# Loading the slices of a first weight with three transfers over 128 partitions in place of four over 32

## Chip, cores and metric

One core of a Trainium2 chip runs the whole kernel. The metric is device time in microseconds (us). Profiles are taken by the hardware profiler, and times in them count from the start of the span, which is some 2 us shorter than the time of a run. PE is the engine of matrix products (PEld is its loading of weights); VectorE (DVE), ScalarE (ACT) and GpSimd (POOL) do the other arithmetic; SP issues the transfers, which 16 DMA engines carry out in packets. A pattern "leads with" the count of its slowest dimension that is not 1.

## The reference

A gated linear attention followed by a feed-forward block. Only the second part touches the change.

```python
# q, k, v, alpha: (4, 8, 768, 48) float32; w_in: (384, 2048), w_out: (2048, 384) float64
for t in range(S):
    state = alpha[:, :, t, :, None] * state + einsum('bhd,bhe->bhde', k[:, :, t], v[:, :, t])
    y[:, :, t] = einsum('bhd,bhde->bhe', q[:, :, t], state)
x = y.transpose(0, 2, 1, 3).reshape(3072, 384)
h = x @ w_in
out = (h * clip(h + 3, 0, 6) / 6) @ w_out
```

The weights come in as float64. The kernel loads the 8 bytes of each number as two 32-bit words and makes float32 of them on ScalarE, VectorE and GpSimd.

## The kernel before

The first weight `w_in` is loaded in eight slices of 256 columns. Row `96 p + 32 t + r` of `w_in` must land in partition `32 p + r` at place `t` (p is a pair of heads, 0 to 3; t is 0 to 2; r is 0 to 31), since the attention leaves x in that order.

```python
    def load_weight(i):
        u = 2 if wide else 1                      # wide: float64 as two words
        dst = weight_dst(i)
        m = dst.shape[1]
        to = raw_of(i).rearrange("p (m n) w -> p m (n w)", m=m) if wide else dst
        if i < NW1:                               # first weight: 8 slices
            n = NSL // KT                         # 256 columns, 2,048 bytes a row
            src = moe_w_in[:, u * i * n : u * (i + 1) * n].rearrange(
                "(p t r) f -> p r t f", p=NP, t=KT)
            for p in range(NP):
                nc.sync.dma_start(out=to[32 * p : 32 * p + 32], in_=src[p])
        else:                                     # second weight: 8 slices, 128 partitions
            o = (i - NW1) * m * C
            nc.sync.dma_start(
                out=to, in_=moe_w_out[o : o + m * C, :].rearrange("(f p) n -> p f n", p=C))
    # ... cut: d1, d2, dx (ScalarE), d3 (VectorE), d4 (GpSimd) turn slice i into float32
```

A hand-made list of words fixes the order in which every engine's work is issued. `w.7` loads slice 7, `d1.7` to `d4.7` convert it, `f.1.7.2` is a product that uses it, `lq.4` loads a tile of q, and `tq.4` transposes it on PE.

```
... w.5 f.0.3.2 sm.3 fg.0.0 ... w.6 f.1.0.0 ... w.7 ca.5 r.5 f.1.2.3 ... d4.5 ... lq.4 fr.0.3 fa.2.0 d3.6 w.8 ...
d3.7 w.9 fr.0.5 tq.4 fr.0.2 f.1.6.3 q.4 d4.7 fg.0.2 d2.8 fg.0.5 d1.8 lk.4 p.5 f.1.7.2 ...
```

## Time and profile before

| | before |
|---|---|
| time, median of 3 runs | 565.23 us (563.75 to 565.41) |
| span of the profiled run | 561.2 us |
| PE busy | 553.9 us, 99% |
| first weight | 8 slices of 786,432 bytes, 4 transfers each, last packet ends at 58.6 us |

(The prediction puts the end of the last packet at 58.9 us. Its times of packets lie some 0.24 us late against the start of the span; here and below they are counted anew from the traces. Differences between them don't change.)

From the page, the count of DMA packets:

```profile
DMA packets 96972, 52.71 MB, mean 94 GB/s; under 512 B 49936, under 2 KB 90128, under 8 KB 96912
```

And busy time by stretch (columns: stretch, its length, then PE, weight loads, VectorE, ScalarE and GpSimd, each busy us and count; then granted clock, DMA share and GB/s):

```profile
14.00:60.00 46.00, 43.46 (x516) 37.02 (x516) 38.02 (x56) 30.37 (x42) 16.05 (x10) 1.00 1.08 187
60.00:100.00 40.00, 40.00 (x326) 31.17 (x326) 35.32 (x52) 22.11 (x32) 15.62 (x15) 1.00 0.67 188
```

While the first weight comes in, PE stands still for only 2.5 of 46 us; from 60 us on it does not stand still at all.

### The profile page before, as it was taken

To read this page: it belongs to the slowest core of one execution; us is meant where nothing else is said; L and a number is where in the kernel's file an instruction comes from. 1 tells how busy PE (TensorE), PEld (TensorE's weight loads), DVE (VectorE), ACT (ScalarE), POOL (GpSimd) and SP (SyncE) were. 2 spreads that over 40 slices of the span, in tenths; PEclk is the share of its full clock that TensorE was granted. 3 is DMA by queue.
4 is the path that set the end of the run, shared out by engine and by line. 5 is a ranking of instruction groups with operands and counts; after the bars stand their busy time and mean duration, and the time that the engine had idled before them with its cause. 6 is when DMAs were issued, how large, how long until landed. Compare 5 with 4: busy or idle time off the path is not lost.

```text
span 561.2 us, 13170 instructions
## 1 busy us (share of the span) xinstructions
PE 553.9 (99%) x5458; PEld 512.6 (91%) x5458; DVE 475.2 (85%) x796; ACT 198.2 (35%) x350; POOL 52.9 (9%) x70
## 2 busy tenths in 40 slices
PE   8899999999999999999999999999999999999997
PEld 7788886699899999999999999899999999999997
DVE  6977997999999999998899899989899886474580
ACT  1567755102521433222342342322332333341420
POOL 2234344100000000000000001000000010000000
DMA  9999856524204606225442551353242400000000
GB/s 147 182 184 205 214 185 179 119 69 110 62 8 117 150 8 158 73 62 137 111 99 51 154 138 34 86 143 86 82 115 60 113 23 1 8 15 15 1 21 30
DMA packets 96972, 52.71 MB, mean 94 GB/s; under 512 B 49936, under 2 KB 90128, under 8 KB 96912
## 3 DMA queue, kind: packets, MB, share of 16 engines
q1 hardware_dynamic: 90288, 47.15, 37.6%
q10 hardware_dynamic: 6624, 4.72, 2.5%
q8 instruction: 43, 0.70, 0.5%
q14 instruction: 17, 0.14, 0.1%
HBM read 43.71 MB, written 8.13 MB: 92 GB/s over the span
## 4 chain that ended last, share of the span: by engine, by line
PE 92%; SPq 3%; DMA 2%; DVE 1%; ACT 1%; issue 0%; POOL 0%; DVEq 0%
PE m_ps L701 35%; PE m_ps L601 32%; PE m_ps L480 6%; PE sc_ps L346 4%; PE y_ps L449 4%; PE m_ps L518 4%; PE y_ps L459 2%; PE m_ps L491 2%; SPq L256 1%; DMA raw<-in_moe_w_in_dram 1%; PE u_ps L413 1%; SPq L267 0%; PE u_ps L419 0%; PE kb_ps L363 0%; SPq L276 0%
## 5 line engine op out<-in xcount | busy, mean ns | idle before, releaser
L701 PE MATMUL m_ps<-w,g_sb 128*128 128x192 f32 x704 | 121.7, 327 | 0.0
L701 PEld LDWEIGHTS m_ps<-w,g_sb 128*128 128x128 f32 x704 | 113.9, 190 | 1.6 <-issue 0.6
L607 ACT COPY g_sb<-m_ps 128x512 f32<-128x512 f32 x110 | 63.9, 584 | 127.5 <-PE m_ps L601 116.4
L701 PE MATMUL m_ps<-rings,g_sb 128*128 128x192 f32 x528 | 91.5, 327 | 0.0
L701 PEld LDWEIGHTS m_ps<-rings,g_sb 128*128 128x128 f32 x528 | 85.4, 190 | 0.3
L601 PE MATMUL m_ps<-xc,w 128*128 128x128 f32 x640 | 84.3, 279 | 0.1
L496 ACT ACTIVATE r<-g_sb,half 128x512 f32<-128x512 f32 x80 | 57.1, 722 | 73.4 <-DVE g_sb L538 27.5
L601 PEld LDWEIGHTS m_ps<-xc,w 128*128 128x128 f32 x640 | 77.4, 192 | 3.5 <-issue 1.4
L500 DVE SCALAR_TENSOR_TENSOR g_sb<-r,g_sb 128x512 f32<-128x512 f32 x80 | 54.9, 692 | 19.7 <-PE m_ps L701 10.8
L396 POOL TENSOR_TENSOR t<-t,R 128x384 f32<-128x384 f32 x20 | 21.1, 1054 | 359.7 <-DVE t L434 165.8
L601 PE MATMUL m_ps<-xT,raw 128*128 128x128 f32 x400 | 52.4, 277 | 0.0
L601 PEld LDWEIGHTS m_ps<-xT,raw 128*128 128x128 f32 x400 | 48.8, 192 | 0.8 <-issue 0.4
L601 PE MATMUL m_ps<-xT,w 128*128 128x128 f32 x320 | 43.0, 279 | 0.0
L648 DVE TENSOR_TENSOR g_sb<-g_sb 128x512 f32<-128x512 f32 (+1 forms) x55 | 41.5, 790 | 0.1
L601 PEld LDWEIGHTS m_ps<-xT,w 128*128 128x128 f32 x320 | 39.1, 191 | 1.6 <-issue 0.6
L352 DVE TENSOR_TENSOR A<-sc_ps,mask 128x512 f32<-128x512 f32 x48 | 30.8, 682 | 8.3 <-PE sc_ps L346 8.3
L480 PE MATMUL m_ps<-xT,w 128*128 128x256 f32 x144 | 32.4, 380 | 0.0
L601 PE MATMUL m_ps<-xc,raw 128*128 128x128 f32 x240 | 32.3, 278 | 0.0
L315 DVE TENSOR_TENSOR_SCAN R<-t,ones 128x516 f32<-128x516 f32 x24 | 29.3, 1219 | 2.0 <-ACT t L306 1.5
L326 DVE TENSOR_TENSOR_SCAN P<-t 128x516 f32<-128x516 f32 x24 | 30.7, 1279 | 0.2
L538 DVE TENSOR_TENSOR g_sb<-g_sb 128x512 f32<-128x512 f32 x40 | 26.9, 685 | 4.5 <-ACT g_sb L607 4.1
L601 PEld LDWEIGHTS m_ps<-xc,raw 128*128 128x128 f32 x240 | 29.7, 192 | 0.8 <-issue 0.4
(112 smaller groups left out, 699.8 us busy)
## 6 DMA issues: line engine op xcount, KB each, us to landing
raw<-in_moe_w_out_dram SPq DMA_DIRECT2D x8, 768.0 KB, 4.7
t<-in_v_dram SPq DMA_DIRECT2D x48, 96.0 KB, 3.0
raw<-in_moe_w_in_dram SPq DMA_DIRECT2D x24, 192.0 KB, 5.7
out_dram<-oh ACTq DMA_DIRECT2D x44, 96.0 KB, 1.7
qq<-in_q_dram SPq DMA_DIRECT2D x36, 96.0 KB, 2.5
aq<-in_alpha_dram SPq DMA_DIRECT2D x36, 96.0 KB, 2.5
kq<-in_k_dram SPq DMA_DIRECT2D x36, 96.0 KB, 2.5
far<-kq SPq DMA_DIRECT2D x13, 256.0 KB, 2.1
```

The costliest lines, as they stand in the source:

```text
L315: nc.vector.tensor_tensor_scan(out=reverse(R, n - 1, n), data0=reverse(ax, n, n), data1=reverse(ones, n, n), initial=0.0, op0=ALU.mult, op ...
L326: nc.vector.tensor_tensor_scan(out=P_t[j], data0=aX[j % 2][:, 0:n], data1=ini[j % 2], initial=0.0, op0=ALU.mult, op1=ALU.add)
L346: nc.tensor.matmul(sc[h % 2][:, h // 2], K_t[j][r, h // 2], Q_t[j][r, h // 2], start=True, stop=True)
L352: nc.vector.tensor_tensor(out=A_t[j][:, NP * o : NP * (o + 1)], in0=ps_t.pop(("sc%d" % o, j)), in1=mask.unsqueeze(1).to_broadcast([C, NP, ...
L480: nc.tensor.matmul(h[:, f], w1[:, kk, o : o + C], xT_t[g][:, kk], start=(kk == 0), stop=(kk == KT - 1))
L496: nc.scalar.activation(out=to, in_=h, func=AF.Relu, bias=half, scale=1.0 / 6.0)
L500: nc.vector.scalar_tensor_tensor(out=to, in0=r, scalar=1.0, in1=h, op0=ALU.min, op1=ALU.mult)
L538: eng.tensor_tensor(out=out, in0=in0, in1=in1, op=ALU.add if s1 > 0 else ALU.subtract)
L601: nc.tensor.matmul(acc[g][i][:, f * C : (f + 1) * C], spots[w][:, f * C : (f + 1) * C], x_of(g, x), start=(first and f == 0), stop=last, s ...
L607: nc.scalar.copy(out=slots[z], in_=acc[g][i])
L648: nc.vector.tensor_tensor(out=out, in0=in0, in1=in1, op=ALU.subtract)
L701: nc.tensor.matmul(to[g], a, rhs[:, f], start=(first and f == 0), stop=(last and f == HF - 1), skip_group_check=True)
```

## The change

The intent: a transfer over all 128 partitions, so that the load isn't held to the DMA ports that 32 partitions reach (point 1 of the prediction below), and three issues a slice in place of four.

```diff
             src = moe_w_in[:, u * i * n : u * (i + 1) * n].rearrange(
-                "(p t r) f -> p r t f", p=NP, t=KT)
-            for p in range(NP):
-                nc.sync.dma_start(out=to[32 * p : 32 * p + 32], in_=src[p])
+                "(p t r) f -> t p r f", p=NP, t=KT)
+            for t in range(KT):
+                nc.sync.dma_start(out=to[:, t], in_=src[t])
```

What the built program carries for one transfer (counts of the dimensions, slowest first): before, source 32 x 3 x 512 and destination 32 x 3 x 512; after, source **4 x 32** x 512 and destination 128 x 1 x 512. The rows of one t lie in four groups 96 rows apart, so the source can't be written as one run of 128 rows.

## The prediction

> **What bounds the kernel now.** I read the page first (busy shares, then the 40 slices).
>
> ```profile
> span 561.2 us, 13170 instructions
> ...
> PE 553.9 (99%) x5458; PEld 512.6 (91%) x5458; DVE 475.2 (85%) x796; ACT 198.2 (35%) x350; POOL 52.9 (9%) x70
> ...
> PE   8899999999999999999999999999999999999997
> DMA  9999856524204606225442551353242400000000
> GB/s 147 182 184 205 214 185 179 119 69 110 62 8 117 150 8 158 73 62 137 111 99 51 154 138 34 86 143 86 82 115 60 113 23 1 8 15 15 1 21 30
> ```
>
> PE is busy nearly all of the time, so a microsecond in which PE stands still early is a microsecond at the end: no later slack can give it back. The DMA row says where PE can be made to wait. Transfers are dense only in the first six or seven slices (14 us each), and there the row is at 9: the front of the kernel already runs near what its transfers deliver. The changed transfers lie in that front. The view of DMA issues gives their number and size, first the before's own:
>
> ```profile
> raw<-in_moe_w_in_dram SPq DMA_DIRECT2D x24, 192.0 KB, 5.7
> ...
> g_sb<-in_moe_w_in_dram SPq DMA_DIRECT2D x8, 192.0 KB, 7.0
> ```
>
> That is 32 transfers of 196,608 bytes, four to each of 8 slices (786,432 bytes a slice, 6.29 MB in all), every packet 2,048 bytes (one row of a slice), so 96 packets a transfer. In the chain of waits, one slice's transfer is on the path itself, the first:
>
> ```profile
> 14.08 7.58 DMA raw<-in_moe_w_in_dram
> ...
> 21.68 0.97 ACT w L207
> ...
> 25.99 1.86 POOL w L228
> ...
> 27.89 1.60 PE m_ps L491 x12
> ...
> 64.46 7.82 PE m_ps L480 x36
> ```
>
> The words read: the slice lands at 21.7, ScalarE and GpSimd turn its float64 bits into float32, and the first product with it starts at 27.9. After 32 us the chain is PE alone. But the timeline shows that PE is only just behind the last slices:
>
> ```profile
> 59.55 0.95 ACT L207 ACTIVATE w<-raw 128x768 f32<-128x768 f32 x1
> ...
> 65.31 1.47 POOL L228 TENSOR_TENSOR w<-raw 128x768 int32<-128x768 int32 x1 [2.75 <-DVE raw L221]
> ...
> 66.83 5.05 PEld L480 LDWEIGHTS m_ps<-xT,w 128*128 128x128 f32 x24 [0.18 <-POOL w L228]
> ```
>
> The eighth slice's last packet ended at 58.9 (packets of the trace); its conversion starts at 59.55, ends at 66.8, and the weight loads at 66.83 waited 0.18 us for just that. So the eighth slice has no slack: if it lands later by X, PE stands still by nearly X. Two stretches give the speed, one filled by first-weight slices, one by second-weight slices (128 partitions each):
>
> ```profile
> 44.00:48.00 4.00, 4.00 (x35) 3.49 (x34) 2.81 (x6) 3.21 (x8) 1.97 (x2) 1.00 1.17 201
> 84.00:88.00 4.00, 4.00 (x60) 3.17 (x59) 3.32 (x7) 3.04 (x5) 1.80 (x2) 1.00 0.84 246
> ```
>
> The last column is GB/s. Within a slice the trace has 96 packets per about 1.0 us, 197 GB/s; second-weight slices, alone in the queue, 201 to 292 GB/s.
>
> **What the Trainium skill says.** (1) "SBUF — State Buffer", section "Door 1: The DMA port swizzle": a transfer that touches 32 neighbouring partitions reaches 8 of the 16 DMA ports (it lists 189 GB/s for 1 MiB there), 128 partitions reach all. The trace agrees: 197 GB/s, and inside a slice most packets take about 160 ns where a lone one takes 84, as if two engines shared a port. This is surely the change's intent. (2) "DMA: Bandwidth & Descriptors", section "Why a DMA increments its semaphore by 16 and not by 1": a transfer issued from SP runs on k engines, k the largest number up to 16 that divides the slowest dimension (not 1) of both access patterns as the instruction carries them; only these k engines post to the semaphore. (3) The same page's "Rules for kernel authors" warns that an outermost dimension under 16 confines the transfer to that many engines. The trace before agrees with (2): its 433 transfers all lead with 32 or 128, and it holds 6,929 packets of 4 bytes, that is 433 x 16 semaphore writes (and one other). (4) "TensorE: Matmul & The Clock Gate", Part 1, says that PE drops to half clock after some 3.4 us idle; the trace agrees in kind: the first matmuls on the identity take 0.25 us each, later ones 0.12.
>
> **The change part by part.** In the built programs the destination becomes 128 partitions x 512 words, but the source, which skips between the four groups of rows, is carried as 4 x 32 x 512. It leads with 4; before, both sides led with 32. By (2), k = 4: engine p carries group p, and 12 engines have no part in the first weight.
> - Removed: 8 of 32 issues on SP, at 0.43 us (median) each, 3.4 us. SP is waiting for earlier landings most of this stretch, so worth about 0.
> - Same: 3,072 packets of 2,048 bytes. No compute instruction is added, removed or reordered: the order of PE, DVE, ACT and GpSimd is the same but for buffer numbers.
> - Each transfer: 128 packets over 4 engines, 32 each. A packet alone takes 84 ns, and an engine runs them end to end (state copies of 2,048-byte packets later in the trace: one begins every 84 ns on each engine). 32 x 84 = 2.7 us a transfer, 8.1 us a slice, 98 GB/s in place of 197 (4.0 us a slice).
> - The queue on these four engines from 14.5 us, when the first slice's packets start, to the end of the eighth: 8 slices x 8.1 = 64.5 us; between them nine transfers of k, q, v and alpha tiles (q3, k3 and the like, 196,608 bytes each, both halves of a v counted as one, and the last q tile comes after). At the 163 GB/s of the first 14 us each takes 1.2 us on all 16 engines, and the four busy ones serve it in their turn: about 9 x 1.2 = 10.8. Sum 75.3, so the eighth slice ends at 89.8 us. The same sum for before, 32 x 1.0 + 10.8 + 14.5 = 57.3, is 1.6 under the 58.9 seen, so the method holds.
> - On the path: the eighth slice is 31 us later. Its conversion took 7.2 us in before amid other work, some of it will now be done while waiting; alone it is ScalarE 0.93 + DVE 0.69 + 0.69 + 0.96 + GpSimd 1.47, with a second ScalarE pass 5.7. So PE's f.1.7 products move from 67.0 to about 96.5, by 29 to 30 us. The steps before show the same in smaller: slice 1 lands +2, slice 0 +7 (its first product at 37.7 moves by 5), slice 2 puts PE at +13, slice 5 at +19, slice 6 at +24.
> - After it: the second weight (16 engines, paced by conversion, 4 us a slice) starts some 31 us later too, and its last slice has about 3 us of slack before its product, so nothing is added. PE's bursts between waits are 4 us against waits of 5, so it will often be cold; only the last warm-up is not hidden, about 2 us.
> Sum: 565.2 + 29.5 + 2 = about 597.
>
> **The rivals.**
> A. All 16 engines carry it after all (the two patterns are matched in some other way). Then a slice goes at 250 to 290 GB/s, 2.9 us as the second weight's. The first slice lands perhaps 2 to 4 us sooner in a stretch where PE already waits; the rest is hidden, since PE is the chain after 32 us. 560 to 564 us. For it: it is the intent. Against it: the source's leading 4, and the rule that the trace agrees with so far. 12%.
> B. k = 4 at full speed per engine, as summed: about 590 to 605. 50%.
> C. k = 4, and the engines also get in each other's way: engines 0 and 1 would write partitions 0-31 and 32-63, which by (1) are the same 8 ports, in the same order. If two step together, each packet takes the 160 ns seen in before, a slice up to 15.4 us, and the eighth slice ends at 14.5 + 123 + 11 = 148: +90 us, 655. An engine that is four packets (0.34 us) ahead is out of the other's way, and engines in this trace drift by more than that, so I expect a part of it at most. For it: the 160 ns. 30%.
> D. k = 4 but mostly hidden, because PE does other work first: 570 to 585. Against it: PE runs its words in a fixed order, and the 0.18 us wait. 8%.
>
> **Range and chances.** The sum gives 597; some weight of C raises the point to 600. 8 in 10: 578 to 650, from D's upper end to most of C. Faster by over 2% (under 554) would need more than rival A gives: 2%. Within 2%: A and a little of D, 13%. Slower: 85%.
>
> **What would show it.** The page's packet total tells k by itself: 96,972 now; with k = 4 the semaphore packets fall from 32 x 16 to 24 x 4, giving about 96,556; with k = 16 about 96,844. If I am right, GB/s in the slices from 14 to 90 us falls to about 100 to 130, dense transfers reach to 125 us in place of 95, time to landing of the first weight doubles or more (5.7 to over 11 us), and the chain of waits shows the first weight's DMA and its conversion several times between 30 and 97 us, with PE busy 5% less than all. A 2,048-byte packet near 84 ns means B, near 160 means C. I am wrong if the slices run at over 190 GB/s (A), or if they are slow and PE yet starts its products at 67 us (D).

## The result, and the profile after

| | before | after |
|---|---|---|
| time, median | 564.5 us (4 runs) | 594.1 us (593.5 to 594.8, 4 runs) |
| ratio | | 1.0524, 95% interval 1.0500 to 1.0548 |
| span of the profile | 561.2 us | 591.7 us |

Ratios here and below are from runs of the same rounds, and not quite the ratios of the medians quoted. The result is correct and the kernel slower by 5.2%, by the forecast's own mechanism, a fuller queue on four engines. The page of the kernel after:

```profile
span 591.7 us, 13144 instructions
...
PE 561.0 (95%) x5458; PEld 518.7 (88%) x5458; DVE 472.9 (80%) x796; ACT 197.9 (33%) x350; POOL 52.0 (9%) x70
...
PE   8775687999999999999999999999999999999998
...
PEclk9988888999999999999999999999999999999999
DMA  9433337644430071523544255045224230000000
GB/s 146 113 110 108 113 113 195 216 120 122 111 95 8 30 196 36 128 57 93 130 113 95 67 140 141 18 119 139 74 76 106 58 80 8 2 14 21 1 20 28
DMA packets 96556, 52.71 MB, mean 89 GB/s; under 512 B 49520, under 2 KB 89712, under 8 KB 96496
```

Read the last line first. The bytes are the same, but there are 416 packets fewer. Before, the 32 transfers of the first weight each ended in 16 semaphore packets of 4 bytes, 512 in all; 512 - 416 = 96 = 24 x 4. So each of the 24 new transfers runs on four engines. The row of GB/s says the same: from the second slice to the sixth it lies at 108 to 113, where it was 182 to 214. PE's row has its holes in these slices and the seventh, in which the first weight ends, and nowhere after. By stretch:

```profile
14.00:60.00 46.00, 31.20 (x435) 26.76 (x436) 24.03 (x37) 18.69 (x28) 9.27 (x7) 0.91 0.41 112
60.00:100.00 40.00, 28.99 (x138) 24.93 (x135) 20.86 (x31) 16.81 (x22) 8.78 (x6) 0.85 0.49 141
```

PE is busy 43.46 - 31.20 = 12.3 us less in the first stretch and 11.0 us less in the second. Its busy time over the whole span is 7.1 us greater (561.0 against 553.9), since part of its work now runs at a lower granted clock, 0.91 and 0.85 in place of 1.00. Together, 30.4 us: the whole difference of the spans, 30.5. After 100 us nothing is lost and nothing won back.

What PE waited for between 14 and 100 us: it stood still for 25.8 us, against 2.5 before. Of this, 16.1 us (5.07, 5.98 and 5.02) are waits for two tiles of alpha and one of q, which landed late; 7.1 us (3.01, 2.87 and 1.19) are waits for results of ScalarE that stood behind a conversion waiting for its slice; only 1.6 us is a wait for a converted weight.

The chain of waits shows who hands the time over (start, duration, what). Before it was PE alone after 32 us; now:

```profile
40.12 15.16 DMA g_sb<-in_moe_w_in_dram
...
77.59 15.16 DMA rings<-in_q_dram
...
92.88 1.09 PE tq_ps L288 x4
93.97 8.87 PE m_ps L480 x36
...
129.10 11.16 PE m_ps L518 x34
```

The piece of 36 products that holds f.1.6 and f.1.7 starts at 93.97 in place of 64.46, 29.5 us later, and takes 8.87 in place of 7.82 us, 1.05 more. That is all of the 30.5, collected in steps on the way: the same PE instruction is 2.7 us later than before at 23 us of the old time, 6.5 at 30, 13.8 at 43, 22.0 at 53 and 29.0 at 64. A second thing is to be seen here: one piece of the chain is not a weight but a tile of q, 15.16 us from issue to landing. Such a tile uses all 16 engines, but on the four busy ones it queues behind the weight (read from the times: the traces don't name the engine of a packet). In the timeline the eighth slice is at PE's heels at the same point:

```profile
92.40 0.90 ACT L207 ACTIVATE w<-raw 128x768 f32<-128x768 f32 x1 [6.70 <-DMA raw<-in_moe_w_in_dram]
...
95.87 1.47 POOL L228 TENSOR_TENSOR w<-raw 128x768 int32<-128x768 int32 x1 [7.28 <-DVE raw L221]
...
97.39 5.05 PEld L480 LDWEIGHTS m_ps<-xT,w 128*128 128x128 f32 x24 [0.30 <-POOL w L228]
```

The same three instructions stood at 59.55, 65.31 and 66.83 before. ScalarE, which went to it without standing still then, now waits 6.7 us for the slice to land.

### The profile page after: what moved, and what is told of

Same layout as the page of the kernel before. It is cut to its first block, busy times and chain, and to the rows that moved or that the text cites. A ratio compares the mean times of both kernels' runs of the same rounds, so it can differ in the third digit from the quotient of the medians.

```text
span 591.7 us, 13144 instructions
## 1 busy us (share of the span) xinstructions
PE 561.0 (95%) x5458; PEld 518.7 (88%) x5458; DVE 472.9 (80%) x796; ACT 197.9 (33%) x350; POOL 52.0 (9%) x70
## 2 busy tenths in 40 slices
DMA packets 96556, 52.71 MB, mean 89 GB/s; under 512 B 49520, under 2 KB 89712, under 8 KB 96496
## 4 chain that ended last, share of the span: by engine, by line
PE 84%; DMA 7%; SPq 6%; ACT 1%; issue 0%; POOL 0%; ACTq 0%
PE m_ps L701 34%; PE m_ps L601 32%; SPq L174 4%; PE sc_ps L346 4%; PE m_ps L518 4%; PE y_ps L449 3%; PE m_ps L480 3%; DMA g_sb<-in_moe_w_in_dram 3%; DMA rings<-in_q_dram 3%; PE y_ps L459 2%; DMA raw<-in_moe_w_in_dram 2%; SPq L256 2%; PE u_ps L413 1%; SPq L276 1%; PE m_ps L491 0%
## 5 line engine op out<-in xcount | busy, mean ns | idle before, releaser
L701 PE MATMUL m_ps<-rings,g_sb 128*128 128x192 f32 x528 | 91.5, 327 | 0.0
L500 DVE SCALAR_TENSOR_TENSOR g_sb<-r,g_sb 128x512 f32<-128x512 f32 x80 | 54.9, 692 | 19.6 <-PE m_ps L701 10.8
L396 POOL TENSOR_TENSOR t<-t,R 128x384 f32<-128x384 f32 x20 | 19.9, 997 | 360.1 <-DVE t L434 165.7
L601 PEld LDWEIGHTS m_ps<-xT,w 128*128 128x128 f32 x320 | 39.1, 191 | 1.6 <-issue 0.6
L480 PE MATMUL m_ps<-xT,w 128*128 128x256 f32 x144 | 35.5, 405 | 0.0
L480 PEld LDWEIGHTS m_ps<-xT,w 128*128 128x128 f32 x144 | 29.2, 208 | 4.5 <-POOL w L228 0.3
L346 PE MATMUL sc_ps<-q,k 48*128 48x128 f32 x384 | 28.4, 284 | 3.0 <-ACT xT L467 2.9
```

The source lines that it names most:

```text
L346: nc.tensor.matmul(sc[h % 2][:, h // 2], K_t[j][r, h // 2], Q_t[j][r, h // 2], start=True, stop=True)
L480: nc.tensor.matmul(h[:, f], w1[:, kk, o : o + C], xT_t[g][:, kk], start=(kk == 0), stop=(kk == KT - 1))
L500: nc.vector.scalar_tensor_tensor(out=to, in0=r, scalar=1.0, in1=h, op0=ALU.min, op1=ALU.mult)
L601: nc.tensor.matmul(acc[g][i][:, f * C : (f + 1) * C], spots[w][:, f * C : (f + 1) * C], x_of(g, x), start=(first and f == 0), stop=last, s ...
L701: nc.tensor.matmul(to[g], a, rhs[:, f], start=(first and f == 0), stop=(last and f == HF - 1), skip_group_check=True)
```

## The experiments

The theory: the number of engines that a transfer uses follows the leading dimension of its source, and everything else follows from that through a full queue on those engines. The rivals: transfers over 128 partitions cut by t are slow by their shape, whatever the source leads with; a slow path or slow issue for any leading dimension under 16, of any size; and, for the way to PE, that only some of the slices matter.

### The same three transfers with a source that leads with 128

If x is kept in its natural order of rows, row `128 t + s` of `w_in` goes to partition s, and the source of one t is one run of 128 rows. The blocks of y, 32 rows each, are written to other places for that (block b = 3p + kk goes to place b % 4 of tile b // 4); one of y's 12 small products then takes 128 rows in place of 64 and comes last. Core of the edit:

```diff
-                "(p t r) f -> t p r f", p=NP, t=KT)
+                "(t q) f -> t q f", t=KT)
...
-        return ps_t["y%d" % (kk // 2), j][32 * p : 32 * p + 32, kk % 2]
+        t, q = divmod(3 * p + kk, NP)
+        return ps_t["y%d" % (t // 2), j][32 * q : 32 * q + 32, t % 2]
```

> Three transfers of 128 partitions a slice, as in the change, but the rows of x are laid out in their natural order, so that the source is carried as 128 x 512 and leads with 128. Theory (number of engines follows the source's leading dimension): all 16 engines again, packet total 96,844 (24 x 16 semaphore packets), a slice in about 3 us as the second weight's, PE back on its old times or a little earlier: 560 to 564 us. Rival (three transfers over 128 partitions are slow in themselves, by their shape in SBUF or by the arrival of a slice chunk by chunk): stays near 594.

Measured: correct, 564.22 us, ratio to before 1.0013 (0.9998 to 1.0028). From its page:

```profile
DMA packets 96844, 52.71 MB, mean 94 GB/s; under 512 B 49808, under 2 KB 90000, under 8 KB 96784
```

That is the count for 24 transfers on 16 engines, and the loss is gone. Same destination, same number of transfers, same size of packet: the shape in SBUF is not the cause. The 384 packets of the third slice loaded run from 24.84 to 27.69 us, 2.85 us a slice, as expected. The total is at the upper edge of the expectation, which the control explains.

The control keeps this row order with the old four transfers (`"(t p r) f -> p r t f"` in the load):

> Control for the new order of the rows: the same order as rows_three, but the four transfers over 32 partitions of the kernel before. Every theory: 565 us within 0.5%, packet total 96,972, about 197 GB/s in a slice. If it differs, the row order itself costs or gains something and rows_three is to be read against this one.

Measured: correct, 567.43 us, ratio 1.0074 (1.0057 to 1.0092), a miss by a quarter of a per cent. The row order has its own price. The groups of instructions by line and shape, kernel before first, then the control:

```profile
L459 PEld LDWEIGHTS y_ps<-q,t 128*32 128x32 f32 x160 | 3.1, 108 | 4.0 <-issue 4.0
```

```profile
L469 PEld LDWEIGHTS y_ps<-q,t 128*32 128x32 f32 x200 | 7.5, 108 | 4.0 <-issue 4.0
```

Busy times of loads overlap with products, so the price is better read from starts: in the traces, the 20 stretches of these small products, each up to the start of the next other product, sum to 18.0 us in place of 15.1, and each of the widened product's two instructions starts 109 ns after the one before it, where most start after 7 ns. The products of A and v into y take 0.6 us more (26.5 us busy in place of 25.9). That is 3.5 of the 4.0 us. So fast loading is worth 567.43 - 564.22 = 3.2 us against the same row order, and the row order takes it back.

### Two and eight in place of four

A dose test. Six transfers a slice, each of half of the groups, lead with 2 (correct result):

```diff
             for t in range(KT):
-                nc.sync.dma_start(out=to[:, t], in_=src[t])
+                for e in range(2):
+                    nc.sync.dma_start(out=to[64 * e : 64 * e + 64, t],
+                                      in_=src[t][2 * e : 2 * e + 2])
```

> The change with each transfer cut in two, so that the source leads with 2 (2 x 32 x 512): six transfers a slice. Theory: two engines, 32 packets of 84 ns each a transfer, 2.7 us a transfer and 16.1 us a slice; eighth slice lands near 154 us, total about 655 to 660 us, packet total 96,556. Rival (cost by number of issues, or a slow path for any leading dimension below 16 that does not depend on its size): 48 issues in place of 24 at some 0.5 us, 595 to 608 us.

Measured: 656.17 us, ratio 1.1645 (1.1628 to 1.1663). Its page and one line of its timeline:

```profile
span 654.4 us, 13206 instructions
...
DMA packets 96556, 52.71 MB, mean 81 GB/s; under 512 B 49520, under 2 KB 89712, under 8 KB 96496
```

```profile
154.33 1.09 PE L290 MATMUL tq_ps<-ident,rings 128*128 128x128 f32 x4 [20.59 <-DMA rings<-in_q_dram]
```

Two engines for each of 48 transfers give the same 96 semaphore packets. The last packet of the eighth slice ends at 152.3 us, and PE waits 20.6 us for the tile of q behind it. The rival of issue costs would have given some 600.

Eight groups of 16 rows, with the rows in a wrong order (the result is wrong, the work is the same):

```diff
-                "(p t r) f -> t p r f", p=NP, t=KT)
+                "(a t r) f -> t a r f", a=8, t=KT)
```

> Wrong result on purpose (rows in another order): the source leads with 8 (8 x 16 x 512), all else as in the change. Theory: eight engines, 16 packets each, 1.35 us a transfer, 4.0 us a slice, which is the 197 GB/s of the kernel before: 562 to 568 us, packet total 96,652. Rival (a slow path for any leading dimension below 16): near 594.

Measured: 564.39 us, ratio 0.9999 (0.9970 to 1.0028).

```profile
DMA packets 96652, 52.71 MB, mean 94 GB/s; under 512 B 49616, under 2 KB 89808, under 8 KB 96592
```

The packet total is the one foretold for eight engines. This kernel has everything that the change has but for the size of the leading dimension: three transfers, 128 partitions, a leading dimension under 16, and issues of about the same length (599 ns median for its later ones). Its time is that of before within the interval of 0.3% either way. Its loading is not quite as fast: the eighth slice ends 4.3 us later than before, and PE waits 1.8 and 0.8 us for tiles of alpha, which the interval, about 1.6 us either way, can hide in part. So a small cost of this kind isn't excluded, one of the change's size is, and neither the shape nor a slow path that is the same for all small leading dimensions explains the loss; the size of the dimension does. The table takes the end of the eighth slice from the packets of each trace and gives the pace as (end - start - 10.8) / 8, where 10.8 us is the prediction's estimate for the nine other tiles in the queue:

| leading dimension of the source | first packet, end of eighth slice | us a slice | expected |
|---|---|---|---|
| 2 | 14.41, 152.31 | 15.9 | 16.1 |
| 4 (the change) | 14.54, 91.38 | 8.3 | 8.1 |
| 8 | 14.25, 62.93 | 4.7 | 4.0 |
| 32 over 32 partitions (before) | 14.30, 58.62 | 4.2 | 4.0 |

### The change in one slice only

Is the whole queue one bill, or do some slices cost nothing? The load takes the new form `if i == 7` (last slice) or `if i == 1` (the first to be loaded), and the old form for the other seven.

> The change for the eighth slice alone, the other seven as before. Theory (the eighth slice has no slack, and each changed slice costs the queue 8.1 - 4.0 us): its packets begin near 54 us as before and end near 62.5 to 63 in place of 58.9, PE's f.1.7 products move by 3 to 4 us, total 567 to 569 us. Rival (the time is lost by the early slices alone, where PE already waited in the kernel before): within 1 us of before.

> The change for the first slice to be loaded alone (slice 1), the other seven as before. Theory (one queue in order on each engine, full to the end of the eighth slice): the four engines that carry it are 3 to 4 us behind from then on, every later slice lands by that much later, and the last one hands it to PE: 566 to 569 us, as much as only7. Rival (an early delay is made up before the eighth slice): 563 to 565 us.

Measured: the last alone 567.14 us, ratio 1.0067 (1.0051 to 1.0084), that is +3.8 us; the first alone 566.02 us, ratio 1.0049 (1.0036 to 1.0062), +2.7 us. The eighth slice ends at 64.8 us in the former, more than foretold (6.2 us later, not 4), and at 62.2 us in the latter, 3.6 us later. From the timeline of the former:

```profile
70.89 4.18 PEld L487 LDWEIGHTS m_ps<-xT,w 128*128 128x128 f32 x20 [1.66 <-POOL w L235]
```

The wait of 0.18 us has become 1.66. In this stretch (60 to 72 us) PE stands still for 2.5 us, where it did not before: first for the tile of q behind the slice (1.23), then for the slice. The rest of this profile's 3.9 us can't be the eighth slice's: at 28 us, before anything differs, this run was already 1.5 us behind, so single profiles differ by that much in their first part.

An early slice costs nearly as much, but not by the way foretold. The delay put into the queue at 15 us is still there at 60 (the eighth slice ends 3.6 us later), yet PE has already paid for it. It paid most at slice 1 itself, where a result of ScalarE stands behind the conversion of the slice; before, then with slice 1 changed:

```profile
23.17 0.56 PE L419 MATMUL u_ps<-t,kb 128*48 128x48 f32 x16 [0.34 <-ACT kb L368]
```

```profile
25.57 0.56 PE L426 MATMUL u_ps<-t,kb 128*48 128x48 f32 x16 [3.90 <-ACT kb L375]
```

It waits 1.18 us more for a tile of alpha at 56.58 us, and from 60 to 80 us it never stands still: the last slice hands it nothing. So the theory's cost is right (566.0 in 566 to 569), its last step is wrong. The rival that an early delay costs nothing falls. Eight times 2.7 to 3.8 us is 22 to 30 us, about the size of the whole loss; that the slices' costs add up is argued, not shown.

### Can loading be made faster than before?

Two tries. One only reorders the four old transfers of a slice:

```diff
-            for p in range(NP):
+            for p in (0, 2, 1, 3):
```

> The kernel before with the four transfers of a slice in the order of groups 0, 2, 1, 3, so that neighbours in the queue go to different halves of the ports. If ports limit a slice and neighbours overlap at all, a slice takes less than its 4.0 us and the time falls by up to 3 us (561 to 563 us); if each transfer is done on all engines before the next begins, nothing changes (564 us).

Measured: 562.03 us, ratio 0.9976 (0.9964 to 0.9988). The eighth slice ends at 56.9 in place of 58.6 us, and the median packet of the first weight takes 140 ns in place of 159. A small gain, but clear of the noise, and the only kernel here that is faster than before beyond it. The wait for the eighth slice can't account for it, since that was 0.18 us only. In the profiles, one of each kernel and so no more than a hint, PE is 0.5 us ahead at 23 us, just after the first slice, and 0.8 in all. That neighbours on different halves of the ports (point 1 of the prediction) overlap a little is a likely cause; the runs show shorter packets and the earlier end, not the ports.

The other takes the natural row order with one transfer of 128 x 3 x 512 a slice (`"(t q) f -> q t f"`), and orders y's small products by their column of PE:

> Rows in natural order, one transfer of 128 x 3 x 512 a slice, and the small products of y ordered so that neighbours fall into different columns of PE. Theory: a slice in 2.9 us on 16 engines and all ports, 3 us earlier than in rows_four, and most of the 3.5 us that the row order cost PE in rows_four back: 560 to 563 us, packet total 96,972 - 24 x 16 = 96,588. If one transfer is worse than three because conversion can't start on a part (it waits for all three today, too), no change is expected from that. Rival (the gain of fast loading is hidden behind PE): no better than 564 us.

Measured: 563.94 us, ratio 1.0011 (0.9999 to 1.0023). Its packet total is 96,586, as foretold but for 2; seven of the eight slices take 3.1 to 3.5 us (first packet to last), a little over the 2.9 foretold. The time is a miss: 564, not 560 to 563. The reordered products got back little: their stretches sum to 17.7 us in place of 18.0, against 15.1 before. So some 3 us from loading stand against some 3 us of PE time, and the sum is nothing.

## Why the prediction was right

The step that carries the number, four engines at 84 ns a packet with everything else queued behind them, was right. The step from there to PE was right in size and partly wrong in path, as told below.

**k = 4.** The packet total was foretold as 96,556 and is 96,556. The Trainium skill, "DMA: Bandwidth & Descriptors", section "Why a DMA increments its semaphore by 16 and not by 1", which says that k is the largest number up to 16 that divides the slowest dimension of both patterns, agrees with all five values seen here: 2, 4, 8, 16 (leading with 32) and 16 (leading with 128). The destination led with 32 or more in every run, so that its side counts too is the page's word alone.

**84 ns a packet, not 160.** In the trace after, the first weight's packets have a median of 84 ns. So rival B held, and C, which put 160 ns on a packet, did not. Eight slices at 8.3 us in place of 8.1 put the end of the eighth at 91.4 us; the sum said 89.8.

**The way to PE.** Foretold: the eighth slice holds PE, and f.1.7's products start at about 96.5 us. Their weight loads stand at 97.39, but after a wait of only 0.30 us for the conversion. What held PE first is the tile of q, just behind the eighth slice in the queue, which lands at 92.75. The prediction counted such tiles as length of the queue and not as things that PE waits for; yet three of them account for 16.1 of the 25.8 us in which PE stood still. That the number did not suffer is luck in part: tile and slice share the busy engines and arrive within about a microsecond of each other. The steps on the way were foretold by slices: PE 5 us late at the first product of slice 0, then 13, 19 and 24. It was 7.3 late at that product, and the later steps came at tiles: 13.8, 22.0 and 29.0. These are waits by engine and line: us in total, times, longest us.

```profile
PE ta_ps L288 <- DMA rings<-in_alpha_dram: 11.1, 2, 6.0
...
PE tq_ps L288 <- DMA rings<-in_q_dram: 5.3, 2, 5.0
```

**The terms that were off.** The cold clock was put at 2 us after the last wait; the last piece grew by 1.05, the wait of 0.30 included. The 29.5 us of shift agree with the start of that piece, which f.1.6 leads; the weight loads of f.1.7 themselves moved by 30.6 (66.83 to 97.39). Two errors cancel in part there: the slice ended 32.8 us later, not 31, and from its last packet to the end of its conversion it took 6.0 us, 2.2 less than before, where the sum had some 1.5 less. The sum, 597, is 2.9 above the median of 594.1, and the 600 lies 5.9 above it, since rival C was given weight that it did not need.

**After it.** The second weight ends at 122.2 us in place of 91.5 and adds nothing, as foretold (125 in place of 95 was said for the end of the dense transfers). One sign did not come as described: between 30 and 97 us the chain holds a transfer of the first weight once (40.12), not several times, and the tile of q once. Not to be checked: the view of DMA issues gives no time to landing for the kernel after, so the forecast of a doubled landing time stays open in that form; the 15.16 us in the chain are the nearest to it.

**Issues.** Eight issues fewer were said to be worth about 0. The waits above leave nothing for them to have won. The new ones are even longer on SP: 531 ns the shortest and 1,076 the median, where the median was 428, and from 60.93 to 77.55 us SP's issues are the chain itself. That slow issuing is the cause, and not a sign of the full queue, is unlikely: with a leading dimension of 8, issues of 599 ns cost no such time. No run separates the two further.

## What to carry to other kernels

Before reshaping a transfer, write down both access patterns as the instruction carries them and look at the slowest dimension of each side: a wide destination was worth nothing here where the source led with 2 or 4. The packet total of the page, through its semaphore packets, tells how many engines carried it. A slow transfer also holds back every wide one behind it in the queue, so count the whole queue, and look among everything in it for what is waited for first, not at the changed transfer alone. Here more than half of the lost time was spent waiting for tiles that the change did not touch.

## What the Trainium skill lacked or had wrong

- "DMA: Bandwidth & Descriptors": it gives the rule for k and, under "Specifications", about 27 GiB/s for an engine (29 GB/s), but no time of a packet and no transfer on few engines. Here one packet of 2,048 bytes took 84 ns (median), 24.4 GB/s if an engine runs them end to end (the last seven of the first weight in the kernel before begin 80 to 86 ns apart); slices took 15.9, 8.3 and 4.7 us with k of 2, 4 and 8.
- The same page says that a transfer's share waits in ring order on each engine; it does not warn that a transfer on all 16 engines is as late as its share behind a narrow one. A q tile took 15.16 us from issue to landing that way.
- The same page gives no issue time on trn2's SP by shape: 428 ns (median) where the source led with 32, 432 ns with 128, 599 ns with 8.
- "SBUF — State Buffer", section on issuing two DMAs to hit both halves, answers no and lists +6%. The size agrees: here the reordering of four transfers made the stretch of the first weight 4% shorter (42.5 us in place of 44.3). What it lacks is that the order of transfers already in one queue can be had for nothing, for 0.24% of the time here.
